# Last output block of a fused attention and gated-MLP kernel: two column parts summed one after the other, both finished by VectorE, and two loads split into smaller DMAs

## The chip, the cores and the metric

The kernel runs on one core of a Trainium2 chip. The metric is the device time of one execution in microseconds, as the median of several runs. One execution was also recorded by the hardware profiler. All times below that carry a place in the run (for example "at 261.68") are microseconds from the start of that recorded span.

## The reference, cut to what matters

```python
# S = 2048 tokens, D = 512, H = 32 heads of 16, window 256, F = 1792; bf16
xn  = layernorm(x)
q, k, v = split(xn @ wqkv)                      # per head
p   = softmax(where(0 <= i - j < 256, q @ k.T / 4, -1e9))
A   = (p @ v).reshape(S, D) @ wo
B   = ((xn @ w_gate) * (xn @ w_up)) @ w_down
out = x + A + B
```

Each output row is a sum of three terms: the input row x, the attention output times `wo`, and the gated product times `w_down`.

## The kernel before, in words

The 2048 tokens are cut into four chunks `T` of 512 tokens, and each chunk into four blocks `b` of 128 tokens. All weights and all of x are kept in SBUF. `setup` issues their loads on SyncE's queue (SP) in one fixed order: x of the first chunk, `Wqkv`, the halves of `Wg` and `Wu` with x of the second chunk between them, then `Wd` (line 78), `Wo` in one DMA (line 79), and x of the last two chunks in one DMA (line 80). Behind these, SP's queue carries the DMA transposes of the normalised x (`norm_transpose`, line 198), the copies `VS<-V` and the stores of the output (line 443). The queue is in order. A DMA of the built program uses one of eight completion semaphores, and one that takes up a semaphore again waits for the earlier DMA on it.

The body of the kernel is a hand-written order. `run` walks over the steps of the attention (`scores`, `values`, `divide`) and puts other matrix work between them: `fillers` lists that work with a cost for each piece, and `fill(upto)` issues pieces until the running cost reaches `upto`. The list's total cost, less `RESERVE`, is spread over the steps, so that about `RESERVE` of filler work is left to be issued after the last attention step.

The output of one block of 128 tokens is summed in PSUM. `down` adds 14 matmuls of `hT` with `Wd` (f = 0 to 13), `wo` adds four matmuls of the attention output `OT` with `Wo` (c = 0 to 3), and `store` reads the sum with VectorE, adds x, writes bf16 to a tile `y` and issues the store. `ypool` has four buffers. The blocks of the last chunk finish after all attention steps. There, the last piece of `OT` (c = 3) comes late, from the last `divide` (line 377 writes it), and TensorE has matmuls of block 3 to do while it waits.

For the very last block (chunk 3, block 3) the 512 columns are held in two PSUM tiles: `L` with columns 0 to 383 and `psd3` with columns 384 to 511. Every step of `down` issues one matmul of 384 columns and one of 128, in turns, each with a weight load of its own. `add_x` (line 429) adds x to the 128-column part on TensorE by a matmul with an identity matrix. At the end `wo` issues four matmuls of 384 columns and then four of 128. VectorE finishes the 384-column part (line 441) and SP stores it. ScalarE copies the 128-column part (line 439) and issues its store on its own queue.

Of the kernel before, what the change touches and what calls it, by code (L numbers as in the profile page):

```python
# [10 lines left out]
ACT = mybir.ActivationFunctionType  # L11
ALU = mybir.AluOpType
# [12 lines left out]
COPY = dict(act=2.8, dve=3.2)  # L25
# [3 lines left out]
class Kernel:  # L29
# [26 lines left out]
    def setup(self):  # L56
        nc, const, NT, NF = self.nc, self.const, self.NT, self.NF
        self.x = const.tile([128, NT, 512], BF16, name="x")
        self.Wqkv = const.tile([128, 4, 1536], BF16, name="Wqkv")
        self.Wo = const.tile([128, 4, 512], BF16, name="Wo")  # L60
        self.Wg = const.tile([128, 4, self.F], BF16, name="Wg")
        self.Wu = const.tile([128, 4, self.F], BF16, name="Wu")
        self.Wd = const.tile([128, NF, 512], BF16, name="Wd")
        xv = self.x_d.rearrange("(t p) d -> p t d", p=128)
        wq = self.w_d["qkv"].rearrange("(k p) n -> p k n", p=128)
        wg = self.w_d["g"].rearrange("(k p) n -> p k n", p=128)
        wu = self.w_d["u"].rearrange("(k p) n -> p k n", p=128)
        for lo, hi in ((0, 1), (1, 2), (2, 4)):
            nc.sync.dma_start(out=self.x[:, lo:hi, :], in_=xv[:, lo:hi, :])
        for lo in (1024, 512, 0):  # L70
            nc.sync.dma_start(out=self.Wqkv[:, :, lo:lo + 512], in_=wq[:, :, lo:lo + 512])
        h = self.F // 2
        for lo in (0, h):
            nc.sync.dma_start(out=self.Wg[:, :, lo:lo + h], in_=wg[:, :, lo:lo + h])
            nc.sync.dma_start(out=self.Wu[:, :, lo:lo + h], in_=wu[:, :, lo:lo + h])
            if lo == 0:
                nc.sync.dma_start(out=self.x[:, 4:8, :], in_=xv[:, 4:8, :])
        nc.sync.dma_start(out=self.Wd[:], in_=self.w_d["d"].rearrange("(f p) n -> p f n", p=128))
        nc.sync.dma_start(out=self.Wo[:], in_=self.w_d["o"].rearrange("(c p) n -> p c n", p=128))
        nc.sync.dma_start(out=self.x[:, 8:NT, :], in_=xv[:, 8:NT, :])  # L80

        warm = const.tile([128, 1], F32, name="warm")
        nc.vector.memset(warm[:], 0.0)
        nc.scalar.activation(out=warm[:], in_=warm[:], func=ACT.Exp)
        self.idle = const.tile([128, 128], BF16, name="idle")
        nc.vector.memset(self.idle[:], 0.0)
        self.keep_busy(40)
        ident = const.tile([128, 128], BF16, name="ident")
        nc.gpsimd.memset(ident[:], 0.0)
        nc.gpsimd.affine_select(out=ident[:], in_=ident[:], compare_op=ALU.not_equal, fill=1.0,  # L90
                                base=0, pattern=[[-1, 128]], channel_multiplier=1)
        self.ident = ident
        pi = const.tile([128, 1], I32, name="pi")
        nc.gpsimd.iota(pi[:], pattern=[[0, 1]], base=0, channel_multiplier=1)
        podd = const.tile([128, 1], I32, name="podd")
        nc.vector.tensor_scalar(out=podd[:], in0=pi[:], scalar1=4, scalar2=1,
                                op0=ALU.arith_shift_right, op1=ALU.bitwise_and)
        self.odd = const.tile([128, 1], F32, name="odd")
        nc.vector.tensor_copy(out=self.odd[:], in_=podd[:])
        self.mhalf = const.tile([128, 4], F32, name="mhalf")  # L100
        nc.gpsimd.memset(self.mhalf[:], -0.5)
        self.diag = const.tile([128, 64], BF16, name="diag")
        self.far = const.tile([128, 64], BF16, name="far")
        nc.gpsimd.memset(self.diag[:], BIG)
        nc.gpsimd.memset(self.far[:], BIG)
        for half in (slice(0, 64), slice(64, 128)):
            self.triangle(self.diag[half], True)
            self.triangle(self.far[half], False)
        self.xnT, self.Q, self.hT, self.O, self.OT = {}, {}, {}, {}, {}
        self.K, self.Ko, self.V, self.VS = {}, {}, {}, {}  # L110
        self.strips, self.parts, self.at = {}, {}, {}
        self.stock = []
        self.new_values()
# [287 lines left out]
        nc.vector.tensor_tensor(out=self.hT[T][:, f, :], in0=ps[:], in1=self.gsb[:], op=ALU.mult)  # L401
        self.book("dve", COPY["dve"])

    def down(self, T, b, lo, hi):

        nc = self.nc
        if lo == 0:
            if T == self.NCH - 1 and b == 3:
                last = self.ps_m.tile([128, 128], F32, tag="M", name="psd3")
                self.sums[b] = [(self.late[3][:, 0:384], 0, 384), (last[:], 384, 512)]  # L410
            elif T == self.NCH - 1 and b == 2:
                self.sums[b] = [(self.late[2][:], 0, 512)]
            else:
                self.sums[b] = [(self.ps_m.tile([128, 512], F32, tag="M", name="psd")[:], 0, 512)]
        for f in range(lo, hi):
            for ps, c0, c1 in self.sums[b]:
                nc.tensor.matmul(ps, lhsT=self.hT[T][:, f, 128 * b:128 * b + 128],  # L417
                                 rhs=self.Wd[:, f, c0:c1], start=(f == 0), stop=False)

    def wo(self, T, b, cs):  # L420
        for ps, c0, c1 in self.sums[b]:
            for c in cs:
                self.nc.tensor.matmul(ps, lhsT=self.OT[T][:, c, 128 * b:128 * b + 128],  # L423
                                      rhs=self.Wo[:, c, c0:c1], start=False, stop=(c == 3))

    def add_x(self, T, b, part):

        ps, c0, c1 = self.sums[b][part]
        self.nc.tensor.matmul(ps, lhsT=self.ident[:], rhs=self.x[:, 4 * T + b, c0:c1],
                              start=False, stop=False)  # L430

    def store(self, T, b, part=0, on_act=False):

        nc = self.nc
        t = 4 * T + b
        ps, c0, c1 = self.sums[b][part]
        y = self.ypool.tile([128, 512], BF16, tag="y", name="y")[:, 0:c1 - c0]
        if on_act:
            nc.scalar.activation(out=y, in_=ps, func=ACT.Copy)
        else:  # L440
            nc.vector.tensor_tensor(out=y, in0=ps, in1=self.x[:, t, c0:c1], op=ALU.add)  # L441
            self.book("dve", COPY["dve"])
        (nc.scalar if on_act else nc.sync).dma_start(out=self.out_d[128 * t:128 * t + 128, c0:c1], in_=y)


    def fillers(self):


        out = []
        NCH, NF = self.NCH, self.NF  # L450

        def add(cost, f, before=None, after=None):
            out.append((cost, f, before, after))
# [36 lines left out]

        def down(T, b, part=range(0, NF, 2)):
            for lo in part:
                add(2, lambda lo=lo: self.down(T, b, lo, lo + 2))

        def wo(T, b, cs):
            add(len(cs), lambda: self.wo(T, b, cs), None, self.last[T, cs[-1]])
# [22 lines left out]
        T = NCH - 1  # L519
        for b in range(4):  # L520
            down(T, b)
            if b < 3:
                wo(T, b, (0, 1, 2))
        add(1, lambda: self.add_x(T, 3, 1))
        return [(*o, None, None)[:4] for o in out]

    def run(self):
# [1 line left out]
        self.now, self.free = 0, dict(act=0, dve=0)  # L529
        self.setup()  # L530
        NCH, LAG = self.NCH, 2
        RESERVE = 36
        self.first_chunk()
        steps, self.first, self.last = [], {}, {}
        for T in range(NCH):
# [7 lines left out]
        work = self.fillers()  # L543
        total = sum(w[0] for w in work) - RESERVE + SCORES * len(steps) + VALUES * (len(due) - 1)
        spent, n = 0, 0
# [3 lines left out]
        def fill(upto, group):  # L549
            nonlocal spent, n  # L550
            while n < len(work):
                cost, f, before, after = work[n]
                if after is not None and after > valued:
                    break
                if spent + cost / 2 > upto and not any(
                        w[2] is not None and w[2] <= group for w in work[n:]):
                    break
                spent += cost
                self.now = spent
                f()  # L560
                n += 1
# [32 lines left out]
        T = NCH - 1  # L594
# [7 lines left out]
        spent += VALUES  # L602
        divide(len(steps) - 1)
        valued = ready
        fill(spent + 15, -1)
        for b in range(3):
            self.wo(T, b, (3,))
            self.store(T, b)
# [1 line left out]
        assert n == len(work)  # L610
        self.wo(T, 3, (0, 1, 2, 3))
        self.store(T, 3, 0)
        self.store(T, 3, 1, True)


@with_exitstack
# [34 lines left out]
```

## Time and profile before

| What | Before |
|---|---|
| median of 4 runs | 267.04 us (266.94 to 267.34) |
| the profiled execution's own time | 266.94 us |
| its span | 265.2 us |
| time outside the span | 1.74 us |
| TensorE busy | 260.5 us of the span |
| VectorE / ScalarE / GpSimd busy | 178.3 / 174.8 / 114.2 us |
| granted TensorE clock, mean | 0.999 |
| moved by DMA | 15.12 MB |

The table says how full each engine is on the whole span. An engine's share over the span does not say what ends last in a single stage. For that, the chain of waits and the timeline of the last ten microseconds are read. The end of a matmul in such a profile is modelled, and neighbouring matmuls overlap; the spacing of two matmuls is read from their starts.

### The profile page before, as it was taken

How to read it: one execution, taken by the hardware profiler on the slowest of the kernel's cores; microseconds unless marked ns; L12 is line 12 of the kernel's file. 1: busy time of each engine (PE TensorE's matmuls, PEld its weight loads, DVE VectorE, ACT ScalarE, POOL GpSimd, SP SyncE). 2: the span in 40 equal slices, each digit the busy share in tenths (PEclk: the TensorE clock that was granted, in tenths of full speed). 3: DMA queues.
4: the chain of work that ended last, by engine and by line, in shares of the span. 5: the costliest groups of instructions: out<-in, count | busy, mean ns of one | idle time of the engine just before them, and what ended most of it. 6: DMA issues, size and time to landing. Idle time of an engine off the chain costs nothing.

```text
span 265.2 us, 8917 instructions
## 1 busy us (share of the span) xinstructions
PE 260.5 (98%) x3891; PEld 119.5 (45%) x3891; DVE 178.3 (67%) x343; ACT 174.8 (66%) x140; POOL 114.2 (43%) x278
## 2 busy tenths in 40 slices
PE   7999999999999999999999999999999999999994
PEld 7444444444445444444444444444444444444453
DVE  6677898787757667677765867766652676767152
ACT  3467687788556678687755668678766566767500
POOL 6125333336673435334585443435344363344500
PEclk9999999999999999999999999999999999999999
DMA  6999911220131000002022100000100010000002
GB/s 194 377 350 344 269 21 22 23 47 4 20 89 35 22 2 1 2 2 47 2 59 66 40 2 2 0 6 7 41 2 20 25 40 2 2 0 5 1 2 80
DMA packets 19351, 15.12 MB, mean 57 GB/s; under 512 B 7280, under 2 KB 19312, under 8 KB 19312
## 3 DMA queue, kind: packets, MB, share of 16 engines
q1 hardware_dynamic: 18624, 14.23, 18.8%
q8 instruction: 30, 0.49, 0.8%
q10 hardware_dynamic: 688, 0.33, 0.5%
q14 instruction: 9, 0.07, 0.1%
HBM read 9.70 MB, written 2.10 MB: 44 GB/s over the span
## 4 chain that ended last, share of the span: by engine, by line
PE 96%; DVE 1%; DMA 1%; issue 0%
PE up L397 19%; PE gp L386 19%; PE psd L417 17%; PE qkp L245 11%; PE S L301 10%; PE acc L355 7%; PE vp L233 5%; PE psd L423 5%; PE L L417 2%; DMA x<-in_A_x_dram 1%; DVE st L164 1%; PE L L423 1%; PE L L355 0%; PE xTp L204 0%; DVE xn L185 0%; DVE y L441 0%
## 5 line engine op out<-in xcount | busy, mean ns | idle before, releaser
L308 ACT ACTIVATE P<-S 128x2048 bf16<-128x2048 f32 x75 | 140.7, 1876 | 47.4 <-PE S L301 41.0
L153 POOL TENSOR_SCALAR_AFFINE_SELECT P<-P 64x256 bf16<-64x256 bf16 x224 | 98.1, 438 | 128.7 <-ACT P L308 117.6
L397 PE MATMUL up<-xnT,Wu 128*128 128x512 bf16 x224 | 60.0, 381 | 0.0
L386 PE MATMUL gp<-xnT,Wg 128*128 128x512 bf16 x224 | 59.0, 380 | 0.0
L417 PE MATMUL psd<-Wd,hT 128*128 128x512 bf16 (+1 forms) x210 | 51.8, 370 | 0.0
L401 DVE TENSOR_TENSOR hT<-up,gsb 128x512 bf16<-128x512 f32 x56 | 38.5, 687 | 19.5 <-PE up L397 18.0
L332 DVE TENSOR_TENSOR P<-P,diag 128x512 bf16<-128x512 bf16 (+1 forms) x75 | 29.6, 395 | 9.7 <-ACT P L308 9.6
L417 PEld LDWEIGHTS <-hT 128*128 128x128 bf16 x238 | 21.2, 98 | 25.0 <-issue 2.7
L361 DVE STREAM_TRANSPOSE at<-acc 128x512 f32<-128x512 f32 x30 | 19.7, 696 | 18.7 <-PE acc L355 18.7
L386 PEld LDWEIGHTS <-Wg 128*128 128x128 bf16 x224 | 20.7, 98 | 25.6 <-issue 1.9
L397 PEld LDWEIGHTS <-Wu 128*128 128x128 bf16 x224 | 19.9, 98 | 25.0 <-issue 3.3
L301 PE MATMUL S<-Q,Ko 32*64 32x320 bf16 (+4 forms) x720 | 31.0, 261 | 0.0
L301 PE MATMUL S<-Q,K 16*64 16x320 bf16 (+4 forms) x720 | 31.0, 260 | 0.0
L224 ACT ACTIVATE gsb<-gp 128x512 bf16<-128x512 f32 x34 | 20.0, 596 | 15.5 <-PE gp L386 13.5
L245 PE MATMUL qkp<-xnT,Wqkv 128*128 128x512 bf16 x128 | 30.0, 380 | 0.0
L301 PEld LDWEIGHTS <-K 16*64 16x64 bf16 x720 | 12.1, 103 | 31.8 <-issue 31.4
L355 PE MATMUL acc<-P,VS 64*32 64x320 bf16 (+4 forms) x672 | 18.8, 254 | 0.0
L355 PE MATMUL acc<-P,V 64*32 64x320 bf16 (+4 forms) x672 | 18.5, 254 | 0.0
L245 PEld LDWEIGHTS <-Wqkv 128*128 128x128 bf16 x128 | 11.7, 98 | 14.6 <-issue 1.6
L226 DVE CAST gsb<-gp 128x512 bf16<-128x512 f32 x22 | 15.2, 691 | 3.4 <-PE gp L386 2.0
L423 PE MATMUL psd<-Wo,OT 128*128 128x512 bf16 (+1 forms) x60 | 16.5, 370 | 0.0
L355 PEld LDWEIGHTS <-V 64*32 64x32 bf16 x720 | 14.5, 91 | 3.2 <-issue 2.6
(57 smaller groups left out, 197.6 us busy)
## 6 DMA issues: line engine op xcount, KB each, us to landing
out_dram<-y SPq DMA_DIRECT2D x15, 128.0 KB, 1.7
Wg<-in_B_w_gate_dram SPq DMA_DIRECT2D x2, 896.0 KB, 11.3
Wu<-in_B_w_up_dram SPq DMA_DIRECT2D x2, 896.0 KB, 12.3
Wd<-in_B_w_down_dram SPq DMA_DIRECT2D x1, 1792.0 KB, 16.4
Wqkv<-in_A_wqkv_dram SPq DMA_DIRECT2D x3, 512.0 KB, 6.4
x<-in_A_x_dram SPq DMA_DIRECT2D x1, 1024.0 KB, 10.9
VS<-V SPq DMA_DIRECT2D x6, 144.0 KB, 2.6
x<-in_A_x_dram SPq DMA_DIRECT2D x1, 512.0 KB, 11.6
```

The source lines that it names most:

```text
L153: nc.gpsimd.affine_select(out=v, in_=v, pattern=pattern + [[1 if diag else -1, 64]], compare_op=ALU.is_ge if diag else ALU.is_gt, fill=0.0 ...
L224: nc.scalar.activation(out=out, in_=in_, func=ACT.Copy)
L245: nc.tensor.matmul(ps[:], lhsT=self.Wqkv[:, k, lo:lo + 128], rhs=self.xnT[T][:, :, k, :], start=(k == 0), stop=(k == 3))
L301: nc.tensor.matmul(S[64 * par:64 * par + 64, e, col:col + n], lhsT=(self.Ko if par else self.K)[U][rows, c, keys], rhs=self.Q[T][rows, c, ...
L308: nc.scalar.activation(out=P[:, :, 0:col], in_=S[:, :, 0:col], func=ACT.Exp, scale=0.25)
L332: self.nc.vector.tensor_tensor(out=v, in0=v, op=ALU.min, in1=self.diag.unsqueeze(1).unsqueeze(1).to_broadcast([128, 4, n, 64]))
L355: nc.tensor.matmul(accs[par][32 * e:32 * e + 32, q:q + n], lhsT=v, rhs=P[rows, e, col:col + n], start=(i == 0), stop=(i == len(todo) - 1), ...
L386: nc.tensor.matmul(ps[:], lhsT=self.Wg[:, k, 128 * f:128 * f + 128], rhs=self.xnT[T][:, :, k, :], start=(k == 0), stop=(k == 3))
L397: nc.tensor.matmul(ps[:], lhsT=self.Wu[:, k, 128 * f:128 * f + 128], rhs=self.xnT[T][:, :, k, :], start=(k == 0), stop=(k == 3))
L401: nc.vector.tensor_tensor(out=self.hT[T][:, f, :], in0=ps[:], in1=self.gsb[:], op=ALU.mult)
L417: nc.tensor.matmul(ps, lhsT=self.hT[T][:, f, 128 * b:128 * b + 128], rhs=self.Wd[:, f, c0:c1], start=(f == 0), stop=False)
L423: self.nc.tensor.matmul(ps, lhsT=self.OT[T][:, c, 128 * b:128 * b + 128], rhs=self.Wo[:, c, c0:c1], start=False, stop=(c == 3))
```

## The change

In the last block the two column parts are no longer summed in turns. The list of fillers now holds only the 384-column matmuls of `down` (14 of them, at cost 1.5 for a pair in place of 2). At the end, `wo` finishes the 384 columns, `store` adds x with VectorE and issues the store on SP. Then come 14 `down` matmuls and four `wo` matmuls of 128 columns, and a second `store` by VectorE and SP. The identity matmul, ScalarE's copy and ScalarE's store are gone. `RESERVE` goes from 36 to 31.5, and one `fill(spent + 15)` becomes `fill(spent + 16)`. In `setup`, `Wo` is loaded in four DMAs of 128 KB instead of one, and x of the last two chunks in three DMAs of 256, 256 and 512 KB instead of one.

```diff
@@ setup
-        nc.sync.dma_start(out=self.Wo[:], in_=self.w_d["o"].rearrange("(c p) n -> p c n", p=128))
-        nc.sync.dma_start(out=self.x[:, 8:NT, :], in_=xv[:, 8:NT, :])
+        wo = self.w_d["o"].rearrange("(c p) n -> p c n", p=128)
+        for c in range(4):
+            nc.sync.dma_start(out=self.Wo[:, c, :], in_=wo[:, c, :])
+        for lo, hi in ((8, 10), (10, 12), (12, NT)):
+            nc.sync.dma_start(out=self.x[:, lo:hi, :], in_=xv[:, lo:hi, :])
@@ down
-    def down(self, T, b, lo, hi):
+    def down(self, T, b, lo, hi, part=0):
...
-        if lo == 0:
+        if lo == 0 and part == 0:
...
         for f in range(lo, hi):
-            for ps, c0, c1 in self.sums[b]:
-                nc.tensor.matmul(ps, lhsT=self.hT[T][:, f, 128 * b:128 * b + 128],
-                                 rhs=self.Wd[:, f, c0:c1], start=(f == 0), stop=False)
+            ps, c0, c1 = self.sums[b][part]
+            nc.tensor.matmul(ps, lhsT=self.hT[T][:, f, 128 * b:128 * b + 128],
+                             rhs=self.Wd[:, f, c0:c1], start=(f == 0), stop=False)
@@ wo
+    def wo(self, T, b, cs, part=0):
         ps, c0, c1 = self.sums[b][part]
+        for c in cs:
+            self.nc.tensor.matmul(ps, lhsT=self.OT[T][:, c, 128 * b:128 * b + 128],
+                                  rhs=self.Wo[:, c, c0:c1], start=False, stop=(c == 3))
@@ add_x (removed)
-        self.nc.tensor.matmul(ps, lhsT=self.ident[:], rhs=self.x[:, 4 * T + b, c0:c1],
-                              start=False, stop=False)
@@ store
-        if on_act:
-            nc.scalar.activation(out=y, in_=ps, func=ACT.Copy)
-        else:
-            nc.vector.tensor_tensor(out=y, in0=ps, in1=self.x[:, t, c0:c1], op=ALU.add)
-            self.book("dve", COPY["dve"])
-        (nc.scalar if on_act else nc.sync).dma_start(out=self.out_d[128 * t:128 * t + 128, c0:c1], in_=y)
+        nc.vector.tensor_tensor(out=y, in0=ps, in1=self.x[:, t, c0:c1], op=ALU.add)
+        self.book("dve", COPY["dve"])
+        nc.sync.dma_start(out=self.out_d[128 * t:128 * t + 128, c0:c1], in_=y)
@@ fillers
-                add(2, lambda lo=lo: self.down(T, b, lo, lo + 2))
+                add(1.5 if (T, b) == (NCH - 1, 3) else 2, lambda lo=lo: self.down(T, b, lo, lo + 2))
...
-        add(1, lambda: self.add_x(T, 3, 1))
@@ run
-        RESERVE = 36
+        RESERVE = 31.5
...
-        fill(spent + 15, -1)
+        fill(spent + 16, -1)
...
         self.wo(T, 3, (0, 1, 2, 3))
         self.store(T, 3, 0)
-        self.store(T, 3, 1, True)
+        self.down(T, 3, 0, self.NF, 1)
+        self.wo(T, 3, (0, 1, 2, 3), 1)
+        self.store(T, 3, 1)
```

More of the change, by code (lines that the diff above doesn't have):

```diff
@@ L415, in down, with store @@
         for f in range(lo, hi):
-            for ps, c0, c1 in self.sums[b]:
-                nc.tensor.matmul(ps, lhsT=self.hT[T][:, f, 128 * b:128 * b + 128],
-                                 rhs=self.Wd[:, f, c0:c1], start=(f == 0), stop=False)
[L420 to L426, printed above, removed]
+            ps, c0, c1 = self.sums[b][part]
+            nc.tensor.matmul(ps, lhsT=self.hT[T][:, f, 128 * b:128 * b + 128],
+                             rhs=self.Wd[:, f, c0:c1], start=(f == 0), stop=False)
+    def wo(self, T, b, cs, part=0):
         ps, c0, c1 = self.sums[b][part]
-        self.nc.tensor.matmul(ps, lhsT=self.ident[:], rhs=self.x[:, 4 * T + b, c0:c1],
-                              start=False, stop=False)
-    def store(self, T, b, part=0, on_act=False):
+        for c in cs:
+            self.nc.tensor.matmul(ps, lhsT=self.OT[T][:, c, 128 * b:128 * b + 128],
+                                  rhs=self.Wo[:, c, c0:c1], start=False, stop=(c == 3))
+    def store(self, T, b, part=0):
         nc = self.nc
```

## The prediction, made before the changed kernel was run

> **What bounds the kernel now.** I read the page first: the busy times, and the shares of the chain that ended last.
>
> ```profile
> PE 260.5 (98%) x3891; PEld 119.5 (45%) x3891; DVE 178.3 (67%) x343; ACT 174.8 (66%) x140; POOL 114.2 (43%) x278
> ...
> PE 96%; DVE 1%; DMA 1%; issue 0%
> ```
>
> TensorE (PE) is busy for 98% of the span and makes 96% of the chain. So a change counts if it changes PE's stream, or the few microseconds before PE starts and after it stops. Then the timeline of the last stage (columns: start, length, engine, line, operation, shapes, count), first where block 3 begins:
>
> ```profile
> 257.00 0.33 PE L417 MATMUL L<-Wd,hT 128*128 128x384 bf16 x1
> 257.17 0.22 PE L417 MATMUL psd<-Wd,hT 128*128 128x128 bf16 x1
> 257.22 0.33 PE L417 MATMUL L<-Wd,hT 128*128 128x384 bf16 x1
> 257.39 0.22 PE L417 MATMUL psd<-Wd,hT 128*128 128x128 bf16 x1
> 257.49 0.61 PE L423 MATMUL psd<-Wo,OT 128*128 128x512 bf16 x2
> 257.93 0.38 PE L423 MATMUL L<-Wo,OT 128*128 128x512 bf16 x1
> 258.15 0.33 PE L417 MATMUL L<-Wd,hT 128*128 128x384 bf16 x1
> ```
>
> By starts, a 384-column matmul takes 0.163 us of PE and a 128-column one 0.055. The matmul at 257.39 should be followed at 257.44, but the next one starts at 257.49: the last piece of OT, which VectorE wrote from 256.72 to 257.43, came just too late. That is a stall of 0.05 us. Then the end:
>
> ```profile
> 260.82 0.81 PE L423 MATMUL L<-Wo,OT 128*128 128x384 bf16 x4
> ...
> 261.47 0.39 PE L423 MATMUL psd<-Wo,OT 128*128 128x128 bf16 x4
> 261.68 0.56 DVE L441 TENSOR_TENSOR y<-L,x 128x384 bf16<-128x384 f32 x1 [1.87 <-PE L L423]
> 261.90 0.28 ACT L439 ACTIVATE y<-psd 128x128 bf16<-128x128 f32 x1 [11.55 <-DMA out_dram<-y]
> 262.20 0.40 ACTq L443 DMA_DIRECT2D out_dram<-y  x1
> 262.26 0.33 SPq L443 DMA_DIRECT2D out_dram<-y  x1
> ```
>
> PE's last start is 261.47 + 3 x 0.057 = 261.64. (In brackets: idle time before, and the inferred releaser.) Both parts of the block are finished side by side, and both stores go out within 0.06 us. The page's DMA issues give the time to landing (last column):
>
> ```profile
> out_dram<-y SPq DMA_DIRECT2D x15, 128.0 KB, 1.7
> ...
> Wd<-in_B_w_down_dram SPq DMA_DIRECT2D x1, 1792.0 KB, 16.4
> ...
> out_dram<-y SPq DMA_DIRECT2D x1, 96.0 KB, 1.7
> out_dram<-y ACTq DMA_DIRECT2D x1, 32.0 KB, 2.0
> ```
>
> The 384-column store lands at 262.26 + 1.7 = 263.96, ScalarE's 128-column store at 262.20 + 2.0 = 264.20. The later one sets the end: 265.2 - 264.2 = 1.0 us of closing follows. So after PE's last start there are 0.26 us to ScalarE's start, 0.30 to its DMA, 2.0 to landing and 1.0 of closing. Last, SP's queue in the first 30 us:
>
> ```profile
> 13.59 8.62 SPq L79 DMA_DIRECT2D Wo<-in_A_wo_dram  x1
> 22.25 1.62 SPq L80 DMA_DIRECT2D x<-in_A_x_dram  x1
> 26.26 2.08 SPq L198 DMA_TRANSPOSE xnT<-xn  x1
> ```
>
> The issue of Wo holds the queue for 8.62 us. SP is free again at 23.87, 2.4 us before the first transpose.
>
> **The change part by part.** *The order before the tail.* The fillers' total loses 7 x 0.5 + 1 = 4.5, and RESERVE loses 4.5, so the work spread over the attention steps is the same. In the built program the order on PE, DVE, ACT and POOL is indeed the same until the matmuls of block 3. I cost this at nothing; nothing moves that would need cover.
>
> *The split loads.* Descriptors and bytes are as before (1 KB rows), and they sit behind Wd in the same queue, so what comes earlier is untouched. SP issues five DMAs more, and each waits for the earlier DMA on its semaphore. The longest of these waits is that of the last x load, which now waits for Wd to land: 11.99 (start of Wd's issue) + 16.4 = 28.4. SP is then free at about 29 to 30 instead of 23.9, and queued behind it is the first transpose of chunk 1, which moves from 26.3 to about 30. The second waits for its xn until 33.19, and the fourth is issued at 48.3, as before. The first reader of these tiles is a weight load at 49.1, so some 15 us hide the delay of the first. x of chunk 2 is first needed long after 33.2 us, when the loads end. Wo is first used behind that too. Cost 0; without that cover it would be up to 4 us. Below nothing it cannot go, since nobody waits for these loads before.
>
> *PE's stream in the tail.* Removed: one identity matmul, 0.055 us. Moved: before the late OT there are now four 384-column matmuls, 4 x 0.163 = 0.65 us from 257.00, so PE reaches the wait at 257.65, after OT is there. The stall of 0.05 goes; what is late next is nothing, since OT then waits for PE. The three `wo` matmuls then end at 258.30, ten `down` matmuls at 259.93, four `wo` matmuls of 384 at 260.58, with the last start at 260.42. The 18 narrow ones follow. The price of one is the open point. The rows show 0.057 us in a row of four (above), each with its own weight load and adding to the same 128 columns, and the eight idle matmuls of 128 columns at 5.45 have 0.056:
>
> ```profile
> 5.40 0.49 PEld L119 LDWEIGHTS <-idle 128*128 128x128 bf16 x8
> 5.45 0.61 PE L119 MATMUL wps<-idle 128*128 128x128 bf16 x8
> ```
>
> (0.61 - 0.22) / 7 = 0.056. Against this speaks the Trainium skill, "TensorE: Matmul & The Clock Gate", section "Back-to-back issue gap": in a stream of weight-load and matmul pairs the spacing is set by both, with some 81 ns at 128 columns. By the rows, 18 x 0.056 = 1.01 us; by the rule, 18 x 0.081 = 1.46, which is 0.45 more and would turn the sum below from a gain into a loss of about 0.15. I take the rows, as these very shapes ran so; the longest row is only eight long, so 0.081 stays in the range, and one weight load's own 0.098 us is the upper end. By the rows the last narrow matmul starts at 260.58 + 17 x 0.056 = 261.53, 0.11 before the old 261.64.
>
> *VectorE.* The 384-column add starts 0.37 after its last matmul's start in the profile (261.68 - 261.31), so now at 260.79, and ends at 261.35; VectorE is free of the three other blocks by about 260. Its store goes out at 261.37 and lands at 263.07, no longer last. The 128-column add starts 0.27 after the last matmul's start (0.37 less 0.11 for the 256 fewer columns that stream; ScalarE's 0.26 is the same), at 261.80. Its length has no row: 512 columns take 0.68, 384 take 0.557, so 0.123 per 128 columns, and 0.557 - 2 x 0.123 = 0.31; the lower end is 0.28, that of ScalarE's copy of the same tile. It ends at 262.11. It also waits for the buffer of the first of the last four stores to come free, but that store was issued at 258.6 and landed in 1.7. Its DMA goes to SP, where the issue of the 384-column store (0.33) ended at 261.7; DMA issue at 262.13.
>
> *The last store.* Removed is ScalarE's DMA; added is one of the same 32 KB on SP. The bounds are 1.7 (SP's rows, the same at 128 and at 96 KB) and 2.0 (the same 256-byte rows, on ScalarE's queue). The Trainium skill, "DMA: Bandwidth & Descriptors", section "Specifications", says that pieces under 512 bytes are written by read-modify-write; if the 0.3 us come from that, they stay, and the gain is 264.20 - 264.13 = 0.07. If they belong to the queue, it is 264.20 - 263.83 = 0.37. Of the 0.3, 0.07 is the longer issue (0.40 against 0.33). For the rest no row decides, and I give half to each: 1.8 us, landing at 263.93, with the closing 1.0 as before.
>
> *Sum.* 264.20 - 263.93 = 0.27 us less: 0.055 for the identity matmul, 0.05 for the stall, and about 0.2 for the shorter landing, less some 0.03 for the longer VectorE step. The profiled execution would go from 266.94 to 266.67. The median of the runs lies 0.10 above that execution, so the forecast is 267.04 - 0.27, or 266.75 rounded.
>
> **The rivals.** What a measurement of this kernel can tell from no change is about 0.2%, or 0.53 us; my forecast is inside it.
>
> *A: a larger gain.* Before, the two last stores were in flight together, and block 2's store, close behind two others, took 2.2 us. If stores lengthen each other, the last one, now alone and 0.75 us behind the other, lands in about 1.5 us. With a 128-column add of 0.28 that gives 262.10 + 1.5 = 263.6, a gain of 0.6: 266.45, and down to 266.2 if the closing is shorter without ScalarE's queue. Against it: the 96 KB store, in flight with the other, took only 1.7.
>
> *B: slower, the narrow matmuls are paced by their weight loads.* All 128-column matmuls of the block now stand in one row at the very end, each with its own load, where before a 384-column matmul covered every second load. At 0.098 us each the row takes 18 x 0.042 = 0.76 more, and with a landing of 2.0 the end is at 264.13 + 0.76 = 264.89, 0.69 later: 267.73. It turns from gain to loss at a spacing of about 0.071. Against it are the two rows above.
>
> *C: SP's queue.* If the semaphore waits among the split loads hold SP until 49 us, the transposes of chunk 1 come late and PE stalls at the projection of chunk 1. This would need Wd to land 20 us later than it did; then each microsecond beyond is one of time, for instance 268.
>
> *D: the change does nothing to see.* If the ScalarE store was not the last to be waited for and the narrow store takes 2.0, PE's 0.1 is all there is: 266.95.
>
> **How the numbers follow.** The forecast with its own range (266.55 to 266.95, D at its upper edge) has 0.48, A 0.32, B 0.17 and C 0.03. A lies mostly beyond the 0.53 us, and a small part of the forecast's case too, so faster has 0.33. B goes over the bound only if the loads are nearly unhidden or if the store is slow as well; with C, and for what I may have missed at the end of the run, slower has 0.17. The rest, 0.50, is within. The range takes in the forecast, most of A and B up to the rule's 0.081 with a landing of 2.0: 267.04 + 0.45 = 267.5. It is 266.2 to 267.5.
>
> **What would show it.** Right: the 18 narrow matmuls are spaced by 0.056 and start at about 260.6; no gap of PE ahead of the late `wo`; VectorE's 384-column add at 260.8 and the 128-column one at 261.8 with 0.3; the last store out at 262.1 and landed within 1.8; the first reader of chunk 1's tiles still at 49.1. Wrong: a spacing of 0.07 or more (B), a landing of 1.5 (A) or above 2.0, or any shift of PE's stream between 30 and 257 us, which I hold for unchanged.

## The result, and the profile after

The changed kernel takes 266.33 us (median of 36 runs, 266.14 to 267.94) against 267.03 us before (57 runs). The ratio is 0.9977, with a 95% interval of 0.9971 to 0.9982: 0.23% faster, which is 0.6 us by the ratio (0.5 to 0.8 by its interval) and 0.7 us between the medians. The profiled execution took 266.36 us; its span is 264.4 us, 0.8 less than before.

The page of the kernel after, same parts as before (busy times; shares of the chain that ended last):

```profile
PE 260.2 (98%) x3890; PEld 119.2 (45%) x3890; DVE 178.5 (68%) x344; ACT 174.5 (66%) x139; POOL 114.2 (43%) x278
...
PE 97%; DVE 1%; DMA 1%; issue 0%
```

Nothing has changed in what bounds the kernel. The timeline of the last stage of the kernel after (start, length, engine, line, operation, shapes, count, and in brackets the idle time before and its releaser):

```profile
257.01 0.81 PE L420 MATMUL L<-Wd,hT 128*128 128x384 bf16 x4
257.66 0.60 PE L426 MATMUL psd<-Wo,OT 128*128 128x512 bf16 x2
...
259.94 0.81 PE L426 MATMUL L<-Wo,OT 128*128 128x384 bf16 x4
260.58 0.95 PE L420 MATMUL psd<-Wd,hT 128*128 128x128 bf16 x14
260.79 0.56 DVE L435 TENSOR_TENSOR y<-L,x 128x384 bf16<-128x384 f32 x1 [0.82 <-PE L L426]
261.37 0.39 PE L426 MATMUL psd<-Wo,OT 128*128 128x128 bf16 x4
261.79 0.29 DVE L435 TENSOR_TENSOR y<-psd,x 128x128 bf16<-128x128 f32 x1 [0.45 <-PE psd L426]
```

PE goes from the four 384-column matmuls to the late OT without a gap: 257.01 + 4 x 0.163 = 257.66. The 14 narrow matmuls from 260.58 to 261.37 are spaced by 0.79 / 14 = 0.056 us. PE's last start is 261.37 + 3 x 0.057 = 261.54. VectorE finishes the wide part while PE still works, and the narrow part in 0.29 us. The DMA issues of the kernel after (queue, number, size, time to landing):

```profile
out_dram<-y SPq DMA_DIRECT2D x15, 128.0 KB, 1.7
...
out_dram<-y SPq DMA_DIRECT2D x1, 96.0 KB, 1.6
out_dram<-y SPq DMA_DIRECT2D x1, 32.0 KB, 1.4
```

This is the line that matters. The last store, out at 262.1, lands in 1.4 us, where the last one before took 2.0. Last, SP's queue in the timeline of the kernel after, and SP's wait for Wd in its list of waits (total, times, longest):

```profile
11.82 1.29 SPq L78 DMA_DIRECT2D Wd<-in_B_w_down_dram  x1
13.15 11.31 SPq L81 DMA_DIRECT2D Wo<-in_A_wo_dram  x4
24.51 5.26 SPq L83 DMA_DIRECT2D x<-in_A_x_dram  x3
29.89 19.65 SPq L201 DMA_TRANSPOSE xnT<-xn  x4
```

```profile
SPq L83 <- DMA Wd<-in_B_w_down_dram: 3.7, 1, 3.7
```

The last x load does wait for Wd, for 3.7 us, and the first transpose moves to 29.9. Its first reader still starts at 49.1.

**A ruler for single executions.** The first loads land at different times in different executions, and PE's whole stream shifts with them. So each profile is read from the start of the first scores matmul (13.43 before, 13.44 after). "PE's stream" is from there to PE's last matmul start; "tail" is from that start to the end of the span. Here the spans are read from the traces to 0.01 us.

| Kernel | first scores at | PE's stream | tail | span |
|---|---|---|---|---|
| before | 13.43 | 248.21 | 3.57 | 265.21 |
| after | 13.44 | 248.10 | 2.87 | 264.41 |
| e1 loads only | 13.59 | 248.21 | 3.43 | 265.23 |
| e2 tail only | 13.52 | 248.10 | 3.13 | 264.75 |
| e3 last store on ScalarE's queue | 14.04 | 248.11 | 2.92 | 265.07 |
| e4 both stores on SP | 13.80 | 248.22 | 3.66 | 265.68 |
| e5 after again | 13.77 | 248.10 | 2.88 | 264.75 |
| e6 one more load | 13.46 | 248.11 | 2.97 | 264.54 |
| e7 wide store held | 13.34 | 248.12 | 3.52 | 264.98 |
| e8 in turns, both by VectorE | 13.56 | 248.16 | 3.65 | 265.37 |

The start varies by 0.7 us among executions. PE's stream does not vary: it has the same length to 0.02 us in all kernels with the same matmuls. The change takes 0.11 from it and 0.70 from the tail.

### The profile page after: what moved, and what is told of

Read it like the earlier page. It is cut to its first block, busy times and chain, and to the rows that moved or that the text cites. A ratio compares the mean times of both kernels' runs of the same rounds, so it can differ in the third digit from the quotient of the medians.

```text
span 264.4 us, 8919 instructions
## 1 busy us (share of the span) xinstructions
PE 260.2 (98%) x3890; PEld 119.2 (45%) x3890; DVE 178.5 (68%) x344; ACT 174.5 (66%) x139; POOL 114.2 (43%) x278
## 4 chain that ended last, share of the span: by engine, by line
PE 97%; DVE 1%; DMA 1%; issue 0%
PE up L400 19%; PE gp L389 19%; PE psd L420 17%; PE qkp L248 11%; PE S L304 10%; PE acc L358 7%; PE vp L236 5%; PE psd L426 5%; PE L L420 2%; DMA x<-in_A_x_dram 1%; DVE st L167 1%; PE L L426 1%; PE L L358 0%; PE xTp L207 0%; DVE xn L188 0%; DVE mv L168 0%
## 5 line engine op out<-in xcount | busy, mean ns | idle before, releaser
L420 PE MATMUL psd<-Wd,hT 128*128 128x512 bf16 (+1 forms) x210 | 49.7, 370 | 0.0
```

## The experiments

Twelve kernels were run: e1 to e4 together on one chip, e5 to e8 together, e9 to e12 together, each group with its own runs of the kernel before. The theories named in the expectations are: "queue" (ScalarE's queue made the old last store slow), "company" (two stores going out at once lengthen each other), "size" (a smaller store lands sooner), "loads", and "semaphores" (the closing waits).

**e1: the loads alone.** The kernel before, with this edit:

```diff
-        nc.sync.dma_start(out=self.Wo[:], in_=self.w_d["o"].rearrange("(c p) n -> p c n", p=128))
-        nc.sync.dma_start(out=self.x[:, 8:NT, :], in_=xv[:, 8:NT, :])
+        for c in range(4):
+            nc.sync.dma_start(out=self.Wo[:, c, :], in_=wo[:, c, :])
+        for lo, hi in ((8, 10), (10, 12), (12, NT)):
+            nc.sync.dma_start(out=self.x[:, lo:hi, :], in_=xv[:, lo:hi, :])
```

> The kernel before with only the loads of Wo and of the later x blocks split into seven DMAs; the tail is as before. My theory: the loads are worth nothing, so 267.0 (within 0.1 of before), with SP held until about 29 by the wait for Wd and the first reader of chunk 1's tiles still at 49.1. The rival that a part of the 0.7 us comes from the loads would give 266.7 or less.

Measured: 266.95 us against 267.09, ratio 0.9997 (0.9988 to 1.0005). Alone the loads are worth nothing that the times can tell. SP waits 3.3 us for Wd, and PE's stream is untouched. In the trace the tail is 0.14 shorter than before (3.43 against 3.57), in the main for a reason that e2 brings out.

**e2: the tail alone.** The kernel after, with the two old load lines.

> The kernel after with the loads put back to two DMAs; the new tail stays. My theory: the whole gain is here, 266.3 to 266.4. The rival (loads carry a part): 266.6 or more.

Measured: 266.74 us against 267.09, ratio 0.9987 (0.9981 to 0.9994). This missed my 266.3 to 266.4. PE's stream is as in the kernel after, so the difference is in the tail, 3.13 against 2.87. SP's own instructions at the end show a part of it: its waits for the semaphores before it closes the kernel (EVENT_SEMAPHORE), then a DRAIN. Durations are in ns as min/median/max. First a stretch of e2, then one of the kernel after:

```profile
L638 SPq EVENT_SEMAPHORE  x7: 17/28/1102, 262.6 to 264.7; - x7
L638 SPq DRAIN  x3: 7/7/13, 264.0 to 264.3; - x3
```

```profile
L641 SPq EVENT_SEMAPHORE  x1: 28/28/28, 263.6 to 263.6; - x1
...
L641 SPq DRAIN  x3: 7/7/13, 263.6 to 264.0; - x3
```

In e2 the long wait, 1102 ns from 262.6, is for the last store, and SP gets to its drain at 264.0, 0.3 after the landing, since it still has other semaphores to go through, though they are long done. In the kernel after the last store's semaphore is the last one to be waited for, and the drain follows the landing by 0.1. The five additional DMAs of the loads move every later DMA on by five of the eight semaphores, which decides the place. In the kernel before, three waits stand behind that of the last landing; in e1 it is one, so most of e1's shorter tail, 0.1 us, is of this kind.

**e3: the last store on ScalarE's queue.** The kernel after, with

```diff
-        nc.sync.dma_start(out=self.out_d[128 * t:128 * t + 128, c0:c1], in_=y)
+        queue = nc.scalar if part else nc.sync
+        queue.dma_start(out=self.out_d[128 * t:128 * t + 128, c0:c1], in_=y)
```

> The kernel after, but the last store (32 KB, 128 columns) is issued on ScalarE's queue instead of SP's; VectorE still makes y, and the store goes out alone, 0.75 us behind the other. Theory 'queue' (ScalarE's queue, unused since 13.5 us, makes the store slow): it lands in 2.0 again, end at about 264.1 + 1.0 in the profile, 266.9. Theory 'company' (two stores going out within 0.06 us lengthen each other, in either queue): it lands in 1.4 to 1.5, 266.4.

Measured: 266.57 us against 267.09, ratio 0.9983 (0.9976 to 0.9990). The DMA issues of e3:

```profile
out_dram<-y SPq DMA_DIRECT2D x1, 96.0 KB, 1.6
out_dram<-y ACTq DMA_DIRECT2D x1, 32.0 KB, 1.5
```

On the same queue, as idle since 13 us as before, the store lands in 1.5 when it goes out alone. "Queue" falls by the landing; the time lies between the two forecasts.

**e4: both stores on SP.** The kernel before, with

```diff
-        (nc.scalar if on_act else nc.sync).dma_start(out=self.out_d[128 * t:128 * t + 128, c0:c1], in_=y)
+        nc.sync.dma_start(out=self.out_d[128 * t:128 * t + 128, c0:c1], in_=y)
```

> The kernel before, but ScalarE's 128-column part is stored from SP's queue, behind the 384-column store: issues at 262.26 and about 262.6. Theory 'queue': it lands in 1.4, at 264.0, 0.2 before the old 264.2, so 266.8. Theory 'company': it lands in about 2.0, at 264.6, so 267.4.

Measured: 267.06 us against 267.09, ratio 0.9999 (0.9991 to 1.0007), between the two forecasts. SP issues the stores one behind the other, so the narrow one is out at about 263.1, 0.42 behind the wide one, and lands in 1.5:

```profile
out_dram<-y SPq DMA_DIRECT2D x1, 96.0 KB, 1.7
out_dram<-y SPq DMA_DIRECT2D x1, 32.0 KB, 1.5
```

So "company" as I had put it falls too: 0.42 us apart on one queue, the narrow store is hardly lengthened. What the shorter landing gives, the later issue takes back.

**e5: the kernel after, again**, beside e6 to e8.

> The kernel after, unchanged, beside the three below on one chip, since the tail alone came out 0.4 us slower than the kernel after had on another chip. Theory 'semaphores' (which position the last store's semaphore has among SP's closing waits is worth some 0.2 us, and the number of load DMAs decides the position): 266.3 to 266.4 here too, below the tail alone. Rival 'another chip': 266.7, like the tail alone.

Measured: 266.52 us against 267.03, ratio 0.9982 (0.9973 to 0.9990), between the two forecasts. Its tail, 2.88, is that of the kernel after, and 0.25 shorter than e2's. The ratios of e5 and e2, each to the kernel before on its own chip, have intervals that overlap. So the traces show that the loads and the new tail together have a shorter end than the new tail alone, and the times agree in sign, but a size for it in the times is not settled.

**e6: one more load.** The kernel after, with

```diff
-        for lo, hi in ((8, 10), (10, 12), (12, NT)):
+        for lo, hi in ((8, 10), (10, 12), (12, 14), (14, NT)):
```

> The kernel after with x of the last two chunks loaded in four DMAs instead of three; this only moves every later DMA on by one of the eight semaphores, so that the last store's is no longer the last to be waited for at the closing but one of the first. Theory 'semaphores': after the last landing SP still has about four waits to go through, 0.3 us to its drain instead of 0.1, so 0.2 slower than the kernel after: 266.5. Rival 'the split loads themselves help': as the kernel after, 266.3.

Measured: 266.57 us against 267.03, ratio 0.9980 (0.9972 to 0.9989): the kernel after in all but 0.05 us, which the runs cannot tell apart. The end of SP, in three stretches of it:

```profile
L641 SPq EVENT_SEMAPHORE  x1: 962/962/962, 262.7 to 262.7; - x1
...
L641 SPq EVENT_SEMAPHORE  x1: 28/28/28, 263.7 to 263.7; - x1
L641 SPq DRAIN  x1: 7/7/7, 263.8 to 263.8; - x1
```

The long wait is now in the middle of the row: two short ones stand before it, two behind. From the end of the long wait to the drain it is 0.16 us by the records' own nanoseconds, and the tail is 0.1 longer than e5's. I had expected four waits behind it and 0.2. The mechanism is seen, at about 0.06 us for a wait; in the time of this kernel it is too small to measure.

**e7: the wide store held back.** The kernel after, with

```diff
+        if (T, b, part) == (self.NCH - 1, 3, 0):
+            self.held = y
+            return
         nc.sync.dma_start(out=self.out_d[128 * t:128 * t + 128, c0:c1], in_=y)
+        if part == 1:
+            nc.sync.dma_start(out=self.out_d[128 * t:128 * t + 128, 0:384], in_=self.held)
```

> The kernel after, but SP issues the 384-column store behind the 128-column one instead of 0.75 us ahead of it: at 262.1 and 262.45, the 96 KB store being last. Both theories of the landing (size, company) give 1.7 for the 96 KB store, at 264.15, so 266.9 to 267.0: the gain of the early wide store is undone. For the 128-column store, 'size' says 1.4, 'company' 1.7 to 2.0. The rival that the wide store's place is worth nothing says 266.4.

Measured: 267.27 us against 267.03, ratio 1.0003 (0.9995 to 1.0012). The timeline and the DMA issues of e7:

```profile
262.04 0.33 SPq L440 DMA_DIRECT2D out_dram<-y  x1
262.42 0.42 SPq L442 DMA_DIRECT2D out_dram<-y  x1
...
out_dram<-y SPq DMA_DIRECT2D x1, 96.0 KB, 1.7
out_dram<-y SPq DMA_DIRECT2D x1, 32.0 KB, 1.4
```

PE and VectorE work as in the kernel after, but the wide store now ends last, and the whole gain of the time is gone. The narrow store, with the wide one 0.38 behind it, lands in 1.4, as it does alone: on one queue it is "size", not "company".

The DMA packets show where company does come in (queue, packets, MB, share of the DMA engines' time; q1 is SP's queue, q10 ScalarE's). First the kernel before from 263.05 to 263.70, then e7 from 262.85 to 263.15 and from 263.30 to 263.80:

```profile
q1 hardware_dynamic: 144, 0.10, 49.4%
q10 hardware_dynamic: 144, 0.03, 23.3%
...
q1 hardware_dynamic: 144, 0.03, 51.8%
...
q1 hardware_dynamic: 144, 0.10, 62.3%
```

In the kernel before, the packets of both last stores move in the same stretch, and those of the 32 KB are spread over 0.48 us. In e7 the wide store's packets begin when the narrow store's have ended, and those of the 32 KB take 0.27 us. They take 0.27 us in e4 and e8 as well, where the two stores' packets do not overlap either, and in e3 on q10. This spread is 0.2 of the 0.5 us that lie between the old store's landing and e3's; 0.1 lies ahead of its first packet and 0.2 behind its last, for which the traces name no cause.

**e8: in turns, both parts by VectorE.** The kernel before without the identity matmul, and with

```diff
-        self.store(T, 3, 1, True)
+        self.store(T, 3, 1)
```

> The kernel before with the matmuls still in turns and with its loads, but without the identity matmul, and with both parts finished by VectorE one after the other and both stored by SP. PE ends 0.055 earlier, so the 384-column add ends at 262.19, the 128-column one at 262.5, its store goes out at 262.53 and lands in 1.5 at 264.0: 266.8 to 266.9, about a third of the gain. The rival that leaving ScalarE's copy and store is the whole change: 266.3 to 266.4.

Measured: 267.31 us against 267.03, ratio 1.0007 (0.9998 to 1.0015): slower than forecast, by 0.4. PE's stream is 0.05 shorter, as the removed identity matmul says. The two stores follow each other on SP; the narrow one, out 0.42 behind the wide one, lands in 1.5, and four short semaphore waits follow it. So it goes out at 262.76, not at the 262.53 of my forecast, since SP is busy with the issue of the wide store until 262.67; and the time outside the span, which the next runs are about, is 0.2 longer than before. So leaving out ScalarE's part gives nothing by itself. It pays only with the order in which the wide part is out of the way before the narrow one is done.

**e9 to e12: the time outside the span.** The runs list the span of each execution beside its time. The median of the difference is 1.72 to 1.74 for the kernel before in every group, 1.74 in e1 and 1.73 in e4, but 1.84 in the kernel after (37 executions), 1.98 in e5 and 1.92 to 2.02 in e2, e3, e6, e7 and e8. So between 0.1 and 0.3 us of the shorter span are given back where no view of the profile looks. The amount is not fixed by the kernel alone: the kernel after has 1.84 here and 1.98 as e5. In the first group of kernels ScalarE copies the last part, in the second it does not. e10 gives it something to do:

```diff
         nc.sync.dma_start(out=self.out_d[128 * t:128 * t + 128, c0:c1], in_=y)
+        if part == 1:
+            touch = self.const.tile([128, 1], BF16, name="touch")
+            nc.scalar.activation(out=touch[:], in_=y[:, 0:1], func=ACT.Copy)
```

e11 has such a copy, from OT, ahead of the final `wo`, and e12 is e10 with 448 and 64 columns. e9, the control, is the kernel after unchanged.

> The kernel after, unchanged, as the control of the three below on one chip: span about 264.6, and time outside the span about 1.9, where the kernel before has 1.73.

> The kernel after, with one extra ScalarE instruction: a copy of one column of the last y tile to a tile that nothing reads, at about 262.1. It is off the path of the stores. All kernels so far in which ScalarE copied the last part (before, e1, e4) had 1.73 outside the span, all without it 1.92 to 2.02, so theory 'late ScalarE work' says outside 1.73, span as the control's, 0.2 below the control: 266.2 to 266.3. Rival 'the identity matmul' (those kernels had that too) or chance: outside as the control's, same time as the control.

> As the one above, but the extra ScalarE copy reads the last piece of OT, so it runs at about 257.5, some 5 us earlier. If what counts is how long ScalarE has been idle at the end (it last works at 250.4 in the control), this gives a part of the 0.2 or all of it; if it must be near the end, nothing: as the control.

> The kernel with the late ScalarE copy, with the last block split into 448 and 64 columns instead of 384 and 128. If a 64-column matmul with its weight load is spaced by 0.030 (in proportion to columns), PE ends as before and the shorter VectorE step gives 0.06: 266.2. If the weight loads pace them at 0.056, as the 128-column ones have, the row costs 18 x 0.026 = 0.47 more: 266.7. That is the slow rival's mechanism, at a width where it should decide.

| Kernel | median, us | ratio to before (95%) | outside the span, median |
|---|---|---|---|
| before | 267.20 | | 1.73 |
| e9 control | 266.65 | 0.9975 (0.9964 to 0.9986) | 1.88 |
| e10 late copy | 266.55 | 0.9975 (0.9967 to 0.9984) | 1.86 |
| e11 early copy | 266.53 | 0.9967 (0.9954 to 0.9979) | 1.84 |
| e12 448 and 64 columns | 266.58 | 0.9972 (0.9961 to 0.9983) | 1.83 |

The copies change nothing: "late ScalarE work" falls. The kernels at 1.73 also have the identity matmul and the wide copy, and I did not take these apart, so what the additional 0.1 to 0.3 us outside the span are stays open.

e12 settles the weight loads. Its timeline, and its DMA issues:

```profile
261.10 0.57 PE L420 MATMUL psd<-Wd,hT 128*128 128x64 bf16 x14
261.30 0.62 DVE L435 TENSOR_TENSOR y<-L,x 128x448 bf16<-128x448 f32 x1 [1.19 <-PE L L426]
261.50 0.28 PE L426 MATMUL psd<-Wo,OT 128*128 128x64 bf16 x4
261.84 0.21 DVE L435 TENSOR_TENSOR y<-psd,x 128x64 bf16<-128x64 f32 x1
...
out_dram<-y SPq DMA_DIRECT2D x1, 112.0 KB, 1.7
out_dram<-y SPq DMA_DIRECT2D x1, 16.0 KB, 1.5
```

Fourteen pairs of weight load and 64-column matmul take 261.50 - 261.10 = 0.40 us, 0.029 each. Loads that set the pace at 0.056 or more would have shown. But the version is no better: the narrow row is over so soon that VectorE is still at the wide part, and the wide store's issue on SP runs to about 262.28 and holds up the narrow one; and 16 KB land no sooner than 32. Beside e10, which differs from it only in the columns, its time is the same (266.58 and 266.55).

No version tried beats the kernel after beyond the intervals.

## Why the prediction was right, and where its sum was off

The predicted 266.75 lies 0.42 above the measured 266.33, which is inside the range given. That is partly the luck of a wide range: the forecast gain of 0.27 us is well under half of the 0.70 measured. The change came out as what the prediction called rival A, the larger gain, in its size (0.6, "266.45, and down to 266.2") and, across two queues, for its main reason: two stores in flight together lengthened each other, and the last one now goes out alone.

- *The order before the tail, cost 0.* Right: PE's stream has its old length but for 0.11 us, which is the identity matmul and the stall of the tail.
- *The split loads, cost 0.* Right for PE's stream, which they leave as it was (e1). The step into the late issue was right as well: the last x load waits for Wd, and the first transpose moves from 26.26 to 29.89, forecast "about 30". What the step did not see is that five more DMAs also move the last store's semaphore to the end of SP's closing waits; the traces show up to 0.2 us of shorter waits for that (e2 against the kernel after), and the times cannot fix the amount.
- *PE's stream in the tail, 0.055 + 0.05.* Right to 0.01: the last start is 261.54, forecast 261.53. The step that weighed the Trainium skill ("TensorE: Matmul & The Clock Gate", section "Back-to-back issue gap") decided for the row of the trace (0.056) against the page's 0.081 at 128 columns, and the measured spacing is 0.056. (By the page's figure the loss would have been 0.45 - 0.27 = 0.18, not about 0.15, and with a landing of 2.0 the time 267.4, not 267.5; neither changes the decision.) At 64 columns it is 0.029. This is rival B's end: the pairs do not run at the pace of their loads at these shapes.
- *VectorE.* Right: 260.79 and 261.79 for the starts (forecast 260.79 and 261.80), 0.29 us for the narrow add (forecast 0.31).
- *The last store, 1.8 us.* This is the term that was mis-sized: it measured 1.4, below both of my bounds (1.7 and 2.0). I took SP's landings as independent of the size because 128 and 96 KB have the same 1.7. But that 96 KB store was in company too; where it goes out alone, it lands in 1.6 (kernel after, e2, e3, e5). At 32 KB it is 1.4, in the kernel after, e5, e7 and e9. So the 256-byte rows do not keep a store at 1.7; what they cost is not shown, since no 32 KB with longer rows were stored. The old store's 2.0 is not the rows, nor the queue (e3: 1.5 on ScalarE's queue), nor ScalarE as the writer of `y` (e4: 1.5). It is seen only where the two stores went out within 0.06 us of each other on two queues (before and e1), and there their packets overlap. At 0.38 us or more apart, on one queue, they do not overlap, and no such lengthening is seen (e4, e7, e8: 1.4 to 1.5). So company on two queues is the cause that is left, by exclusion. It was not tried with nothing else changed: e4 moves the store to the other queue and later as well. The prediction's argument against rival A, that the 96 KB store took only 1.7 in company, fails with the 1.6; block 2's 2.2, its argument for it, is no sign of company on one queue, since in the kernel after the same three stores, 0.6 us apart, all land in 1.7.
- *The closing, 1.0 us.* It is 0.9 in the kernel after, by the shorter row of semaphore waits: SP's drain comes 0.08 us behind the last landing, where it came 0.25 behind it before. Rival A looked for a shorter closing too, but in the absence of ScalarE's queue; e3 uses that queue and has the short closing.
- *Outside the span.* I carried it over as 1.74; it is 1.84 at the median of the kernel after. This gives 0.1 back.

With these three terms set right the sum is 0.27 + 0.4 + 0.1 - 0.1 = 0.67 us, against 0.70 between the medians. Rival D (nothing to see) and C (SP's queue held until 49) did not happen; the queue was held until 29.9.

## What to carry to other kernels

When the kernel's end is a chain of last matmul, last copy, last store and closing, make the last store small and let no other store leave with it on another queue: most of the output should be summed, finished and stored while TensorE still has work for the remainder. The remainder need not be as small as possible: it must leave VectorE and the store queue time to be done with the large part (64 columns were no better than 128). Dropping ScalarE's work at the end (e8) or moving its store to SP's queue (e4) gave nothing by itself; the order did.

## What the runs showed of the hardware that I had not expected

- A store of 128 columns lands in 1.4 us when alone, one of 384 in 1.6 to 1.7 and one of 512 in 1.7. The same 32 KB took 2.0 beside a 96 KB store issued 0.06 us later on another queue, with the packets of the two overlapping.
- SP's closing waits go through the semaphores in a row, at about 0.06 us each even where the DMA has long landed, so that the place of the last one is worth up to some 0.2 us. The number of DMAs issued at the start of the kernel decides this place.
- The time outside the span is not a constant of the program's frame: 1.72 to 1.74 in three kernels and 1.83 to 2.02 in the others, for a reason that stays open.
- The start of the first scores matmul varied from 13.34 to 14.04 us between executions, by the landing of the first loads (in these two, the first part of Wqkv landed at 6.38 and 7.13), while everything from there to PE's last start kept its length to 0.02 us in kernels with the same matmuls. A difference of a few tenths is better read from such an anchor than from one span.
